# DeltaNet with a channel mixer on one core: the first channel product of the last batch for 768 tokens at once, in 11 products for 12

## The chip, the core and the metric

The kernel runs on one NeuronCore of a Trainium2 chip. The core has TensorE (PE, matrix products, with its weight loads shown apart as PEld), VectorE (DVE), ScalarE (ACT), GpSimd (POOL), SyncE (SP, which only starts transfers here) and 16 DMA engines. They run side by side and wait for each other by semaphores. TensorE reads SBUF and writes PSUM, which has eight banks of 512 float32 columns; VectorE and ScalarE take results out of PSUM.

The metric is the device time of one execution in microseconds; the median of several runs is given.

## What is computed

Four batches of 768 tokens pass through DeltaNet (8 heads of width 48), and the result, 384 wide, through a mixer:

```python
y[:, :, t] = np.einsum('bhd,bhde->bhe', q[:, :, t], state)      # DeltaNet, for t in range(768)
v_old = np.einsum('bhde,bhd->bhe', state, kt)
state = state + bt[:, :, :, None] * np.einsum('bhd,bhe->bhde', kt, vt - v_old)
...
x = y.transpose(0, 2, 1, 3).reshape(4, 768, 384)
h = x.transpose(0, 2, 1) @ U @ V                                # token mixing, rank 32
u = x + h.transpose(0, 2, 1)
out = u + np.maximum(u @ w_ch1, 0.0) @ w_ch2                    # 384 -> 1536 -> 384
```

The change concerns the last line, for the last batch: `u @ w_ch1`, called the first channel product here. `@ w_ch2` is the second.

## The kernel before

All arithmetic is float32. DeltaNet is computed in units of half a batch, eight in all; the working set of a unit lies in one of two SBUF slots (`slots`, 9792 columns each), units taking them in turn. The mixer takes a batch in three groups of 256 tokens (`GT`, `NG`). For each group:

- `front(b, i)` (line 1030) mixes tokens: `x += v @ tt` (line 1054, 384 columns, summed on VectorE in line 1058), six transposes (line 1062), and a copy by ScalarE into `ut` (line 1065). It works in blocks of 128 tokens.
- `wide(b, i)` (line 1080) makes the first channel product (line 1132): 12 feature blocks of 128, each 3 products of a 128x128 weight block with 256 tokens. Two feature blocks share a PSUM bank, from which `relu` (line 1088) writes `hs`.
- Then it makes the second channel product (line 1169) by the seven products of a Strassen-Winograd scheme, each a sum over 6 weight blocks of 192 columns. `add_up` (line 1104) and `last_sum` (line 1111) make the sums of `hs` that it needs, in `S1`, `S2` and `hs`; the sums of weights were made at the start. `gather` (line 1117) adds results to `X` and starts the store of 128 tokens by SP (line 1121).

The order of instructions isn't written out by hand. Every part is a generator that yields the operations it wants to issue (engine, estimated cost, PSUM banks to take or give back) and the keys it waits for (`need`); `run` (line 209) keeps a clock for each engine and picks the next operation by place, the number that `begin` gives to a part. Fronts have place 2, `wide` 95; a table, `PLACES`, gives other places to some parts. The result is a fixed program with a fixed order on each engine. PSUM is handed out as four `pair`s of two banks; once the first batch is ready the last pair is taken away and split into two single banks, `mix`, for the channel products.

In the last batch no DeltaNet is left to run beside the mixer.

Of the kernel before, what the change touches and what calls it, by code (L numbers as in the profile page):

```python
# [8 lines left out]
FP32 = mybir.dt.float32  # L9
# [10 lines left out]
GT = 256  # L20
# [6 lines left out]
def kernel(  # L27
# [66 lines left out]
    def dve(n):  # L94
        return (n + 151) / 960.0
# [14 lines left out]
    def need(*keys):  # L110
        return [key for key in keys if key[1] >= 0]
# [232 lines left out]
    v_sb = const.tile([128, S], FP32, name="v_sb")  # L344
    w2_sb = const.tile([128, PRODUCTS, HF, HD], FP32, name="w2_sb")
    hs = const.tile([128, FT, GT], FP32, name="hs")
    S1 = const.tile([128, HF, 128], FP32, name="S1")
    S2 = const.tile([128, HF, 128], FP32, name="S2")
    X = const.tile([128, 2, NB, DM], FP32, name="X")
# [574 lines left out]
    def sums(f):  # L924
# [3 lines left out]
            nc.vector.tensor_tensor(out=w[:, to], in0=w[:, a], in1=w[:, c], op=ALU.subtract)  # L928
        emitted(("sums", f), 0.2)

    def load_weights():
        landed = {}
        slices = list(weight_slices())
        room = X.bitcast(I32).rearrange("p a b d -> p a (b d)")[:, 1]
        wides = [
            room[:, 0 : 2 * WIDE],
            conv.tile([128, 2 * WIDE], I32, name="wide", bufs=1),
            hs.bitcast(I32).rearrange("p f n -> p (f n)")[:, 0 : 2 * WIDE],
        ]
        where = [0, 1, 0, 1, 2, 0, 1, 2, 0, 1, 0, 1, 0, 1]  # L940
        uppers, powers = room[:, 2 * WIDE :], conv.tile([128, WIDE], I32, name="power", bufs=1)
# [36 lines left out]

        yield need(("seeded", 0))
        for i in range(len(slices)):  # L980
            begin(start(i), 22)
        for i in range(len(slices)):
            dst, n = slices[i][0], size(i)
            yield need(("wide", i))
            yield op("dve", 0.15 + n / 1850, port=True)
            wide = landed.pop(i)
            h, low = wide[:, :, 1], wide[:, :, 0].bitcast(U32)
            power, upper = powers[:, 0:n], uppers[:, 0:n]
            nc.vector.tensor_scalar(
                out=power, in0=h, scalar1=20, scalar2=0x7FF,  # L990
                op0=ALU.logical_shift_right, op1=ALU.bitwise_and,
            )
# [24 lines left out]
            nc.vector.scalar_tensor_tensor(  # L1017
                out=dst, in0=mant, scalar=2.0 ** -20, in1=power, op0=ALU.mult, op1=ALU.mult
            )
            emitted(("weights", i), 0.1)  # L1020
            if i >= W2 + 4:
                begin(sums(3 * (i - W2 - 4)), 21)

    uts, tts = {}, {}
    NG = S // GT

    def before(b, i):
        return (b, i - 1) if i > 0 else (b - 1, NG - 1)

    def front(b, i):  # L1030
        yield need(
            ("front", *before(b, i)), ("wide", *before(*before(b, i))),
            ("weights", 1), *[("x", b, c) for c in range(NC)],
        )
        x = X[:, b % 2]
# [13 lines left out]
        ut = uts[b, i] = mix.tile([128, KT, GT], FP32, name="ut")  # L1049

        def block(c):
            o = yield op("pe", 0.65, "F", take="pair", words=4)
# [25 lines left out]
        emitted("mixing")  # L1078

    def wide(b, i):  # L1080
        yield need(("front", b, i), ("narrow", *before(b, i)))
        x, ut = X[:, b % 2], uts[b, i]
        if b == 0 and i == 0:
            yield ["mixing"]

# [6 lines left out]
        def part(k, m, f0, n=3):  # L1092
            return hs[:, k * HF + f0 : k * HF + f0 + n, 128 * m : 128 * m + 128]

        def add_up(f0, fs):
            yield need(*[("h", b, i, x) for x in fs])
# [17 lines left out]
        def gather(m, p, c, h, last):  # L1114
            yield op("dve", dve(HD), give=[("mix", m)])
            to = x[:, NT * i + c, HD * h : HD * h + HD]
            nc.vector.tensor_tensor(out=to, in0=to, in1=p, op=ALU.add)  # L1117
            if last:
                yield op("sp", 0.4)
                at = (NT * i + c) * 128  # L1120
                nc.sync.dma_start(out=out[b, at : at + 128, :], in_=x[:, NT * i + c])
                emitted(("stored", b, NT * i + c), 2.0)

        firsts = []
        for y, fs in enumerate(PAIRS):
            yield need(("weights", 2 + y))
            for f in fs:
                got = yield op("pe", 1.3, "F", take="mix" if f == fs[0] else None, words=12)
# [19 lines left out]

        banks = {}
        for y, (w, a, keys, bank, first, c, h, last) in enumerate((  # L1150
            (0, part(0, 0, 0, HF), [("h", b, i, x) for x in ((3, 4), (5, 9))] + [("weights", W2 + 2)],
             0, True, 0, 0, False),
            (1, part(1, 0, 0, HF), [("h", b, i, (10, 11)), ("weights", W2 + 5)], 1, True, 0, 0, False),
            (5, S2, [("summed", b, i, 0), ("summed", b, i, 3), ("sums", 0), ("sums", 3)],
             0, False, 0, 1, False),
            (4, S1, [], 1, True, 1, 1, False),
# [17 lines left out]
            begin(gather(m, p_o, c, h, last), 3)  # L1174
        emitted(("narrow", b, i))

    with tc.manual_schedule():
# [13 lines left out]
                    begin(load(n, name, (0, 1)), FIRST.get((name, n), 20 + 4 * n + y))  # L1191
        begin(load_weights(), 40)
        begin(reserve(), 0)
        for b in range(B):
            for i in range(NG):
                begin(front(b, i), 2)
# [34 lines left out]
```

## Time and profile before

| quantity | value |
|---|---|
| median of 3 runs | 621.54 us (621.28 to 623.51) |
| the profiled execution | 622.19 us |
| its span, first to last instruction | 620.1 us |
| mean granted TensorE clock | 0.939 |
| ScalarE, Relu of line 1088, 128x512 | 72 times, 597 ns |
| VectorE, sum of line 1104, 128x384 | 72 times, 551 to 559 ns |
| VectorE, gather of line 1117, 128x192 | 84 times, 350 ns |
| stores of 192 KB (line 1121), issue to landing | 24 times, median 1.9 us |

The page of a profile gives busy time of each engine, the same in 40 slices of the span, and groups of equal instructions: line, engine, operation, what it writes and reads, how often, busy time and mean, then the idle time of the engine just before such instructions and who ended it. The chain of waits is followed back from the last instruction, at each step to what released it. Timelines list instructions by start and length. The time of an execution is some 2 us longer than its span. TensorE's matrix records overlap, so the pace of a series is read from starts, not from the mean length.

### The profile page before, as it was taken

The numbers are of one execution on the slowest core, as the hardware profiler recorded it, in microseconds if no ns is written. First come the engines' busy times: TensorE is split into PE (matmuls) and PEld (weight loads), VectorE is DVE, ScalarE is ACT, GpSimd is POOL, SyncE is SP. The second block draws the span as 40 slices with busy tenths as digits, with TensorE's granted clock in tenths as the row PEclk, the third lists the DMA queues.
The fourth block names the chain that finished last, engine by engine and source line by source line (L and its number), as shares of the span: only waits on it lengthen the run. The fifth ranks groups of instructions, "written<-read, shape, count | busy, mean of one in ns | idle before, by whom it ended". The sixth has DMA issues, their size and how long they took to land.

```text
span 620.1 us, 23438 instructions
## 1 busy us (share of the span) xinstructions
PE 589.1 (95%) x10536; PEld 518.6 (84%) x10536; DVE 401.0 (65%) x965; ACT 228.3 (37%) x450; POOL 82.5 (13%) x145
## 2 busy tenths in 40 slices
PE   6678988999999999999999999999999999999997
PEld 5578976789888878799889878889889869898987
DVE  5869997898989613889898128898894123131312
ACT  3465564740342553521621643245324321101020
POOL 3011052410010343200100511401001000000000
PEclk9766565999999999999999999999999999999999
DMA  9840568850000332410000611600000000000000
GB/s 146 159 88 5 177 177 177 186 123 14 15 4 29 64 75 52 77 37 0 30 3 13 113 41 30 133 2 3 30 3 14 16 3 9 18 5 21 15 12 25
DMA packets 72004, 33.26 MB, mean 54 GB/s; under 512 B 59616, under 2 KB 70368, under 8 KB 71904
## 3 DMA queue, kind: packets, MB, share of 16 engines
q1 hardware_dynamic: 66112, 24.98, 18.3%
q0 software_dynamic: 4192, 6.49, 4.6%
q8 instruction: 82, 1.34, 0.9%
q10 hardware_dynamic: 1600, 0.30, 0.3%
q14 instruction: 18, 0.15, 0.1%
HBM read 27.03 MB, written 4.72 MB: 51 GB/s over the span
## 4 chain that ended last, share of the span: by engine, by line
PE 82%; DVE 9%; SPq 5%; issue 2%; DMA 1%; ACT 0%; ACTq 0%; DVEq 0%
PE P L1132 30%; PE P L1169 27%; SPq L382 4%; PE P L505 3%; PE P L478 2%; PE P L860 2%; PE P L1054 2%; PE P L775 2%; PE P L888 2%; PE P L811 2%; PE P L789 2%; DVE prod L596 1%; DVE xt L602 1%; PE P L822 1%; PE P L666 1%
## 5 line engine op out<-in xcount | busy, mean ns | idle before, releaser
L1132 PE MATMUL P<-ut,w_sb 128*128 128x256 f32 x864 | 201.9, 385 | 0.0
L1132 PEld LDWEIGHTS P<-ut,w_sb 128*128 128x128 f32 x864 | 159.4, 190 | 22.4 <-issue 0.6
L1169 PE MATMUL P<-w_sb,hs 128*128 128x192 f32 x720 | 125.6, 329 | 0.0
L1169 PEld LDWEIGHTS P<-w_sb,hs 128*128 128x128 f32 x720 | 117.1, 190 | 3.9 <-issue 1.2
L1088 ACT ACTIVATE hs<-P 128x512 f32<-128x512 f32 x72 | 43.0, 597 | 167.1 <-PE P L1132 163.1
L1117 DVE TENSOR_TENSOR X<-X,P 128x192 f32<-128x192 f32 x84 | 29.4, 350 | 62.7 <-PE P L1169 62.1
L602 DVE TENSOR_TENSOR xt<-xt,prod 128x112 f32<-128x112 f32 (+21 forms) x200 | 64.6, 323 | 6.9
L596 DVE TENSOR_TENSOR prod<-gs,xt 128x112 f32<-128x112 f32 (+21 forms) x200 | 64.1, 321 | 4.8
L759 ACT COPY X<-P 64x192 f32<-64x192 f32 x96 | 30.1, 313 | 71.3 <-PE P L789 54.6
L1169 PE MATMUL P<-w_sb,S 128*128 128x192 f32 x288 | 50.5, 329 | 0.0
L1169 PEld LDWEIGHTS P<-w_sb,S 128*128 128x128 f32 x288 | 46.8, 190 | 0.6
L1104 DVE TENSOR_TENSOR S<-hs 128x384 f32<-128x384 f32 x24 | 13.2, 552 | 52.4 <-ACT hs L1088 52.3
L873 DVE TENSOR_TENSOR z<-slot,P 128x192 f32<-128x192 f32 x44 | 15.5, 352 | 45.6 <-PE P L860 30.8
L478 PE MATMUL P<-ident,slot 128*128 128x128 f32 x192 | 30.4, 309 | 13.4 <-DMA slot<-in_k_dram 11.4
L478 PEld LDWEIGHTS P<-ident,slot 128*128 128x128 f32 x192 | 25.0, 158 | 18.3 <-issue 13.2
L731 ACT COPY slot<-zz 32x384 f32<-32x384 f32 x64 | 32.5, 509 | 12.2 <-DVE zz L609 7.9
L493 ACT COPY slot<-P 128x768 f32<-128x768 f32 x30 | 23.7, 803 | 31.1 <-PE P L478 30.9
L581 POOL MEMSET xt<- 128x1056 f32 x8 | 7.8, 980 | 186.7 <-DVE zz L609 186.7
L505 PE MATMUL P<-slot 48*64 48x64 f32 x1536 | 31.8, 238 | 0.5 <-ACT slot L493 0.2
L505 PEld LDWEIGHTS P<-slot 48*64 48x64 f32 x1536 | 28.7, 150 | 3.9 <-ACT slot L493 2.1
L738 POOL MEMSET slot<- 32x384 f32 x32 | 13.6, 424 | 108.6 <-PE P L695 63.0
L382 POOL DMA_DIRECT2D slot<-in_k_dram x36 | 24.2, 679 | 28.1 <-PE P L888 28.1
(119 smaller groups left out, 780.7 us busy)
## 6 DMA issues: line engine op xcount, KB each, us to landing
out_dram<-X SPq DMA_DIRECT2D x24, 192.0 KB, 1.9
slot<-in_k_dram SPq DMA_DIRECT2D x56, 72.0 KB, 4.0
X<-in_moe_w_ch_dram SPq DMA_DIRECT2D x10, 384.0 KB, 5.5
wide<-in_moe_w_ch_dram SPq DMA_DIRECT2D x10, 384.0 KB, 5.1
slot<-in_q_dram SPq DMA_DIRECT2D x40, 72.0 KB, 3.6
slot<-in_v_dram SPq DMA_DIRECT2D x40, 72.0 KB, 2.7
slot<-in_k_dram POOLq DMA_DIRECT2D x36, 72.0 KB, 3.9
slot<-in_q_dram POOLq DMA_DIRECT2D x24, 72.0 KB, 4.6
```

The source lines that it names most:

```text
L382: queue.dma_start(out=t[half(1 - g if name == "z" else g), :, to, 0:D], in_=src[b, 4 * g + s, hf * UC * L : (hf + 1) * UC * L, :].rearrang ...
L478: nc.tensor.transpose(p_t[:, c // 3, c % 3], t[:, c, 2 * j : 2 * j + 2].rearrange("p s d -> p (s d)"), ident,)
L493: nc.scalar.copy(to, p_t)
L505: nc.tensor.matmul(p_g[half(g ^ (par * i)), par, c], kq[rows, c, j, 0, half(g)], kq[rows, c, j, i, half(g)], start=True, stop=True,)
L596: nc.vector.tensor_tensor(out=prod, in0=gb[:, :, j : j + 1, j + 1 :].to_broadcast([128, split, m, w]), in1=xb[:, :, 0:m, j : j + 1].to_bro ...
L602: nc.vector.tensor_tensor(out=xb[:, :, 0:m, j + 1 :], in0=xb[:, :, 0:m, j + 1 :], in1=prod, op=ALU.subtract,)
L731: nc.scalar.copy(pg[quarter(i), :, at, :, a : a + BK], cut(zc, h)[quarter(i)].rearrange("p r (c j) t -> p r c j t", j=2),)
L759: nc.scalar.copy(x[half(c % 2), c // 2, 4 * D * g : 4 * D * (g + 1)].rearrange("p (j r d) -> p r j d", r=2, d=D), states(p_y)[half(g)],)
L1088: nc.scalar.activation(hs[:, fs[0] : fs[1] + 1 : fs[1] - fs[0]], p_f, ACTF.Relu)
L1117: nc.vector.tensor_tensor(out=to, in0=to, in1=p, op=ALU.add)
L1132: nc.tensor.matmul(p_f[:, fs.index(f)], w1_sb[:, y, 256 * t + 128 * fs.index(f) :][:, 0:128], ut[:, t], start=(t == 0), stop=(t == KT - 1),)
L1169: nc.tensor.matmul(p_o, a[:, f], w2_sb[:, w, f], start=(first and f == 0), stop=(f == HF - 1), skip_group_check=True,)
```

## The change

For the last batch, the first channel product is no longer made by group. `first_of_last` waits for the fronts of all three groups, then starts `quick(f)` for f = 0 to 5. Each makes four results of 128 features by 384 tokens: feature blocks f and f + 6 (k = 0, 1), token halves m = 0, 1. The inner dimension has three blocks of 128. Over the first two, 2x2 blocks are multiplied in 7 products for 8; the third adds 4; so 11 products of 384 columns stand for 12. Partial results are copied by ScalarE from PSUM into `hs_last` and added to there by VectorE, and the Relu is then made in place by ScalarE (`cut`), or straight from PSUM for one of the four.

`hs_last` (12 x 768 columns) lies in slot 0 and `ut_last` with the sums of tokens in slot 1, whose units are finished by then. Sums of weights lie in the two buffers used for the conversion of the weights at the start (`converted`, `exponents`), apart from one that takes the place of a weight block. `weight_sums` makes the first 18 of them once all weights are in and the second channel product of batch 1's first group has been issued, and the last six when batch 2 is through its last first product. `token_sums` makes five sums of 384 columns.

The front of the last batch no longer waits for an earlier `wide`. The second channel product is the same, from `hs_last`. For the very last group the results are stored by halves of columns, each as soon as it is final, four transfers for two.

In the built program the order on every engine is as before up to the last batch, apart from the 24 sums of weights on VectorE: 18 stand between lines 618 and 873 soon after the first group of batch 1, six among lines 1046 to 1117 at the end of batch 2. From the fork on, TensorE's order is: the blocks of the last 256 tokens, moved ahead between the last products of batch 2; the 66 products of `quick`; then three times the second channel product, the first of its seven in front of the last two products of `quick`.

```diff
+    LAST = B - 1
+    hs_last = slots[0][:, 0 : FT * S].rearrange("p (f n) -> p f n", f=FT)
+    ut_last = slots[1][:, 0 : KT * S].rearrange("p (t n) -> p t n", t=KT)
+    ts_last = slots[1][:, KT * S : KT * S + 2 * S].rearrange("p (z n) -> p z n", z=4)
+    w1_sums = [converted.bitcast(FP32)[:, 0:WIDE], converted.bitcast(FP32)[:, WIDE:]]
+    w1_sums = [t.rearrange("p (f x) -> p f x", f=HF) for t in w1_sums + [exponents.bitcast(FP32)]]
...
+    def weight_sums():
+        yield need(("weights", W2 + 5), ("narrow", 1, 0))
+        for f in range(HF):
+            a11, a12, a21, a22 = (w1_of(f + HF * k, t) for k in range(2) for t in range(2))
+            n1, s2, s4 = (t[:, f] for t in w1_sums)
+            for to, a, c, sign in ((n1, a21, a22, -1.0), (s2, n1, a11, -1.0), (s4, a12, s2, 1.0)):
+                yield op("dve", dve(128), port=True)
+                nc.vector.scalar_tensor_tensor(
+                    out=to, in0=a, scalar=sign, in1=c, op0=ALU.mult, op1=ALU.subtract
+                )
+        emitted(("w1 sums", 1), 0.1)
+        yield need(("wide", LAST - 1, NG - 1))
+        for f in range(HF):
+            yield op("dve", dve(128), port=True)
+            a21 = w1_of(f + HF, 0)
+            nc.vector.tensor_tensor(out=a21, in0=w1_of(f, 0), in1=a21, op=ALU.subtract)
+        emitted(("w1 sums", 0), 0.1)
...
+    def quick(f):
...
+        def cut(k, m):
+            yield op("act", act(384))
+            nc.scalar.activation(c(k, m), c(k, m), ACTF.Relu)
+            emitted(("cut", k, m, f), 0.06)
+
+        def add(k, m, p, **more):
+            yield op("dve", dve(384), rush=True, **more)
+            nc.vector.tensor_tensor(out=c(k, m), in0=c(k, m), in1=p, op=ALU.add)
+            begin(cut(k, m), 3)
...
+        x = yield op("pe", 0.65, "F", take="pair", words=4)
+        px, pz = (pair(x)[:, z, 0:384] for z in range(2))
+        mm(px, w1_of(f, 0), u(0, 0), start=True, stop=True)
+        begin(copies(), 3)
+        yield need(("tokens", 0), ("w1 sums", 1))
+        yield op("pe", 0.65, "F", words=4)
+        mm(pz, n1, t1, start=True, stop=True)
+        emitted(("fifth", f), 0.22)
+        y = yield op("pe", 1.3, "F", take="mix", words=8)
+        py = mixed(y)[:, 0:384]
+        mm(py, w1_of(f, 1), u(1, 0), start=True)
+        mm(py, w1_of(f, 2), u(2, 0), stop=True)
+        emitted(("other", f), 0.22)
+        begin(first(y), 3)
+        yield need(("begun", f))
+        yield op("pe", 0.65, "F", words=4)
+        mm(px, s2, t2, stop=True)
+        begin(second(), 3)
+        yield need(("third", f))
+        yield op("pe", 1.3, "F", words=8)
+        mm(pz, s4, u(1, 1))
+        mm(pz, w1_of(f, 2), u(2, 1), stop=True)
+        emitted(("both", f), 0.22)
+        begin(both(), 3)
+        yield need(("second", f), ("w1 sums", 0))
+        yield op("pe", 1.3, "F", words=8)
+        mm(px, w1_of(f + HF, 0), u(0, 1))
+        mm(px, w1_of(f + HF, 2), u(2, 1), stop=True)
+        yield from add(1, 1, px)
+        yield op("pe", 1.3, "F", words=8)
+        mm(px, w1_of(f + HF, 1), t4)
+        mm(px, w1_of(f + HF, 2), t5, stop=True)
...
     def wide(b, i):
-        yield need(("front", b, i), ("narrow", *before(b, i)))
-        x, ut = X[:, b % 2], uts[b, i]
+        yield need(("front", b, i), ("half" if b == LAST else "narrow", *before(b, i), *[3] * (b == LAST)))
+        x, hs = X[:, b % 2], hidden
+        if b == LAST:
+            hs = hs_last[:, :, GT * i : GT * i + GT]
+        else:
+            ut = uts[b, i]
...
-            if last:
+            at = (NT * i + c) * 128
+            if b == LAST and i == NG - 1:
+                if final:
+                    yield op("sp", 0.4)
+                    cols = slice(HD * h, HD * h + HD)
+                    nc.sync.dma_start(out=out[b, at : at + 128, cols], in_=x[:, NT * i + c, cols])
+            elif last:
                 yield op("sp", 0.4)
-                at = (NT * i + c) * 128
                 nc.sync.dma_start(out=out[b, at : at + 128, :], in_=x[:, NT * i + c])
...
-        for y, fs in enumerate(PAIRS):
+        if b == LAST:
+            for f0 in range(0, HF, 3):
+                begin(add_up(f0, ()), 4)
+            yield need(("narrow", *before(b, i)))
+        for y, fs in enumerate(PAIRS if b < LAST else ()):
```

In the order of `quick`, the small letters of the code stand for these products of a block f, in the order in which they are issued: A is the first (into `px`), B the one with `n1` (into `pz`), then the two into `py`, E the one with `s2`, F the two with `s4` and `w1_of(f, 2)`, G the two in front of `add(1, 1, px)`, H the two behind it.

More of the change, by code (lines that the diff above doesn't have):

```diff
@@ L346 @@
     hs = const.tile([128, FT, GT], FP32, name="hs")
+    hidden = hs
     S1 = const.tile([128, HF, 128], FP32, name="S1")
@@ L929, in sums @@
         emitted(("sums", f), 0.2)
+    converted = conv.tile([128, 2 * WIDE], I32, name="wide", bufs=1)
+    exponents = conv.tile([128, WIDE], I32, name="power", bufs=1)
     def load_weights():
@@ L936, in load_weights @@
             room[:, 0 : 2 * WIDE],
-            conv.tile([128, 2 * WIDE], I32, name="wide", bufs=1),
+            converted,
             hs.bitcast(I32).rearrange("p f n -> p (f n)")[:, 0 : 2 * WIDE],
@@ L940, in load_weights @@
         where = [0, 1, 0, 1, 2, 0, 1, 2, 0, 1, 0, 1, 0, 1]
-        uppers, powers = room[:, 2 * WIDE :], conv.tile([128, WIDE], I32, name="power", bufs=1)
+        uppers, powers = room[:, 2 * WIDE :], exponents
         def size(i):
@@ L1022, in load_weights, with w1_of @@
                 begin(sums(3 * (i - W2 - 4)), 21)
+    LAST = B - 1
[4 more added lines that the diff above has]
+    w1_sums = [t.rearrange("p (f x) -> p f x", f=HF) for t in w1_sums + [exponents.bitcast(FP32)]]
+    def w1_of(f, t):
+        y = [f in fs for fs in PAIRS].index(True)
+        return w1_sb[:, y, 256 * t + 128 * PAIRS[y].index(f) :][:, 0:128]
@@ new lines, in token_sums @@
+    def token_sums():
+        yield need(*[("front", LAST, i) for i in range(NG)])
+        u = ut_last.rearrange("p t (m n) -> p t m n", m=2)
+        t1, t2, t4, t5 = (ts_last[:, z] for z in range(4))
+        for to, a, c, how in (
+            (t1, u[:, 0, 0], u[:, 0, 1], ALU.subtract),
+            (t2, u[:, 1, 1], t1, ALU.add),
+            (u[:, 0, 1], u[:, 1, 1], u[:, 0, 1], ALU.subtract),
+            (t4, u[:, 1, 0], t2, ALU.subtract),
+            (t5, u[:, 2, 0], u[:, 2, 1], ALU.subtract),
+        ):
+            yield op("dve", dve(384), port=True)
+            nc.vector.tensor_tensor(out=to, in0=a, in1=c, op=how)
+        emitted(("tokens", 0), 0.1)
@@ new lines, in quick, with u, c, mm @@
+    def quick(f):
+        n1, s2, s4 = (t[:, f] for t in w1_sums)
+        t1, t2, t4, t5 = (ts_last[:, z] for z in range(4))
+        def u(t, m):
+            return ut_last[:, t, 384 * m : 384 * m + 384]
+        def c(k, m):
+            return hs_last[:, f + HF * k, 384 * m : 384 * m + 384]
+        def mm(to, w, t, start=False, stop=False):
+            nc.tensor.matmul(to, w, t, start=start, stop=stop, skip_group_check=True)
+        def cut(k, m):
[6 more added lines that the diff above has]
+            begin(cut(k, m), 3)
+        def first(y):
+            yield need(("begun", f), ("other", f))
+            yield from add(0, 0, py, give=[("mix", y)])
+        def copies():
+            yield op("act", act(384), rush=True)
+            nc.scalar.copy(c(0, 0), px)
+            emitted(("begun", f), 0.06)
+            yield need(("fifth", f))
+            yield op("act", act(384), rush=True)
+            nc.scalar.copy(c(1, 1), pz)
+            emitted(("third", f), 0.06)
+        def second():
+            yield op("act", act(384), rush=True)
+            nc.scalar.copy(c(0, 1), px)
+            emitted(("second", f), 0.06)
+        def both():
+            yield need(("both", f), ("second", f))
+            yield from add(0, 1, pz)
+            emitted(("out", f))
+        x = yield op("pe", 0.65, "F", take="pair", words=4)
[30 more added lines that the diff above has]
+        mm(px, w1_of(f + HF, 2), t5, stop=True)
+        emitted(("quick", f))
+        yield op("act", act(384), rush=True)
+        nc.scalar.activation(c(1, 0), px, ACTF.Relu)
+        emitted(("cut", 1, 0, f), 0.06)
+        yield need(("out", f))
+        free["pair"][x] = state["now"] + 0.06
@@ L1024, with first_of_last @@
+    def first_of_last():
+        yield need(*[("front", LAST, i) for i in range(NG)], ("narrow", LAST - 1, NG - 1))
+        for f in range(HF):
+            begin(quick(f), 94)
     uts, tts = {}, {}
@@ L1031, in front @@
         yield need(
-            ("front", *before(b, i)), ("wide", *before(*before(b, i))),
+            ("front", *before(b, i)), *[("wide", *before(*before(b, i)))] * (b < LAST),
             ("weights", 1), *[("x", b, c) for c in range(NC)],
@@ L1048, in front @@
         cs = list(range(i * GT // 128, (i + 1) * GT // 128))
-        ut = uts[b, i] = mix.tile([128, KT, GT], FP32, name="ut")
+        if b < LAST:
+            ut = uts[b, i] = mix.tile([128, KT, GT], FP32, name="ut")
+        else:
+            ut = ut_last[:, :, GT * i : GT * i + GT]
         def block(c):
@@ L1080, in wide @@
     def wide(b, i):
-        yield need(("front", b, i), ("narrow", *before(b, i)))
-        x, ut = X[:, b % 2], uts[b, i]
+        yield need(("front", b, i), ("half" if b == LAST else "narrow", *before(b, i), *[3] * (b == LAST)))
+        x, hs = X[:, b % 2], hidden
+        if b == LAST:
+            hs = hs_last[:, :, GT * i : GT * i + GT]
+        else:
+            ut = uts[b, i]
         if b == 0 and i == 0:
@@ L1093, in part, with cut_off @@
             return hs[:, k * HF + f0 : k * HF + f0 + n, 128 * m : 128 * m + 128]
+        def cut_off(ks, fs):
+            ms = ((0,), (0, 1), (1,))[i]
+            return [("cut", k, m, f) for k in ks for m in ms for f in fs] if b == LAST else []
         def add_up(f0, fs):
-            yield need(*[("h", b, i, x) for x in fs])
+            yield need(*[("h", b, i, x) for x in fs], *cut_off(range(2), range(f0, f0 + 3)))
             at = slice(f0, f0 + 3)
@@ L1112, in last_sum, with gather @@
             emitted(("summed", b, i, 6), 0.1)
-        def gather(m, p, c, h, last):
+        def gather(m, p, c, h, last, final):
             yield op("dve", dve(HD), give=[("mix", m)])
@@ L1150, in wide @@
         for y, (w, a, keys, bank, first, c, h, last) in enumerate((
-            (0, part(0, 0, 0, HF), [("h", b, i, x) for x in ((3, 4), (5, 9))] + [("weights", W2 + 2)],
+            (0, part(0, 0, 0, HF),
+             cut_off((0,), range(HF)) or [("h", b, i, (3, 4)), ("h", b, i, (5, 9)), ("weights", W2 + 2)],
              0, True, 0, 0, False),
-            (1, part(1, 0, 0, HF), [("h", b, i, (10, 11)), ("weights", W2 + 5)], 1, True, 0, 0, False),
+            (1, part(1, 0, 0, HF),
+             cut_off((1,), range(HF)) or [("h", b, i, (10, 11)), ("weights", W2 + 5)],
+             1, True, 0, 0, False),
             (5, S2, [("summed", b, i, 0), ("summed", b, i, 3), ("sums", 0), ("sums", 3)],
@@ L1173, in wide @@
             emitted(("half", b, i, y))
-            begin(gather(m, p_o, c, h, last), 3)
+            begin(gather(m, p_o, c, h, last, y in (1, 4, 5, 6)), 3)
         emitted(("narrow", b, i))
@@ L1193 @@
         begin(reserve(), 0)
+        begin(weight_sums(), 97)
+        begin(token_sums(), 3)
+        begin(first_of_last(), 94)
         for b in range(B):
```

## The prediction

> **What bounds the kernel now.** I read the page first (busy shares, then the slices), then the chain of waits, then the timelines of the last 120 us, then the last transfer.
>
> ```profile
> PE 589.1 (95%) x10536; PEld 518.6 (84%) x10536; DVE 401.0 (65%) x965; ACT 228.3 (37%) x450; POOL 82.5 (13%) x145
> PEclk9766565999999999999999999999999999999999
> ...
> L1132 PE MATMUL P<-ut,w_sb 128*128 128x256 f32 x864 | 201.9, 385 | 0.0
> ```
>
> TensorE is busy 95% of the span, it runs at full clock from the ninth slice on, and the matmuls of the first channel product (line 1132) have no idle time in front of them. The records come in twos: one product in the code gives two passes, each with its own weight load. The chain of waits from 500 us on shows where the change sits:
>
> ```profile
> 519.61 7.80 PE P L1169 x48
> 527.41 15.54 PE P L1132 x72
> 542.95 1.29 PE P L1054 x4
> 544.24 1.95 PE P L1169 x12
> 546.19 0.65 PE P L1062 x6
> 546.84 11.70 PE P L1169 x72
> 558.55 15.54 PE P L1132 x72
> 574.09 13.65 PE P L1169 x84
> 587.74 15.54 PE P L1132 x72
> 603.28 13.66 PE P L1169 x84
> 616.94 0.02 issue
> 616.97 0.35 DVE X L1117
> ```
>
> Each row is start, length, what. From 507 to 617 us the path is TensorE alone: one piece starts where the last ended. Three first products of 256 tokens (line 1132) take 15.54 each. The page's mean of 385 ns is no price, since records overlap. The pace is 15.54/72 = 0.2158 us for a pass of 256 columns, 1.95/12 = 0.1625 for 192 columns, 1.29/4 = 0.3225 for 384 columns (line 1054). So time removed from TensorE here is time off the end, if nothing new makes it wait. The two other engines are mostly idle there:
>
> ```profile
> 520.00:540.00 20.00, 20.00 (x106) 18.48 (x105) 3.01 (x7) 2.56 (x5) 0.00 (x0) 1.00 0.05 20
> 580.00:600.00 20.00, 20.00 (x106) 18.53 (x105) 3.33 (x8) 2.39 (x4) 0.00 (x0) 1.00 0.06 20
> ```
>
> (PE, weight loads, VectorE, ScalarE, GpSimd, clock.) Three rows of the timelines give the price of a handover:
>
> ```profile
> 590.41 0.60 ACT L1088 ACTIVATE hs<-P 128x512 f32<-128x512 f32 x1 [15.63 <-PE P L1132]
> 504.61 0.35 DVE L873 TENSOR_TENSOR z<-slot,P 128x192 f32<-128x192 f32 x1 [1.75 <-PE P L860]
> 505.02 0.45 PE L789 MATMUL P<-z,slot 64*64 64x48 f32 x16 [0.24 <-DVE z L873]
> ```
>
> The first pair of blocks ends its 12 passes at 587.74 + 12 x 0.2158 = 590.33, and ScalarE starts 0.08 later. VectorE ends at 504.96 and TensorE starts 0.06 later. A mean record of 0.385 at a pace of 0.216 has 0.17 of drain; the chain's starts already stand after it, but I add it once, to be safe. The round trip TensorE, ScalarE, TensorE for 384 columns is then at most 0.17 + 0.08 + 0.48 (line 488, 480 ns) + 0.06 = 0.79 us, and over VectorE with 0.55 (line 1058) 0.86.
>
> **What the skill says.** "TensorE: Matmul & The Clock Gate", section "Back-to-back issue gap", gives columns/2.4 GHz plus 2.5 ns. The trace agrees, with two cycles a column for each of the two float32 passes: 256 x 2/2.4 + 2.5 = 215.8 ns, 384 columns 322.5. Its "Step-by-step: what each phase is for" says that weight loads are pulled ahead of running matmuls; a load has 190 ns here, under the 322 of the new passes. "DMA: Bandwidth & Descriptors", in "Anatomy of one DMA", makes most of a small transfer a fixed cost of about 2 us; the 192 KB stores land in 1.9, so that order holds. "SBUF — State Buffer", section "Who interferes with whom", says that a VectorE instruction with two SBUF inputs gets in the way of GpSimd instructions that read SBUF, not of those that only write. The trace agrees for issuing: four POOL transfers at 397.25 took 2.62 us beside such VectorE work, 0.66 each, as everywhere.
>
> **The change part by part.**
>
> *The product.* Removed: 3 x 72 passes at 0.2158 = 46.62 us. Added: 6 blocks x 11 products x 2 passes = 132 passes at 0.3225 = 42.57. Both are path. **Gain 4.05.** The pace of 384 columns is measured on four passes only; drawn on from 192 and 256 columns it would be 0.2158 + 2 x 0.0533 = 0.3224, so the bounds lie within 0.1 us in all.
>
> *New waits in the product.* The order of TensorE's instructions is unchanged up to the last batch-2 product. Then a block f stands in the queue as A (1 product), B (1), H of the block before (2), other (2), E (1), F (2), G (2). G accumulates on what ScalarE copies out after E: between lies F, four passes, 4 x 0.3225 = 1.29 against 0.79: 0.50 to spare. H needs VectorE's sum after G: A and B lie between, 1.29 against 0.86: 0.43 to spare. E and F wait on copies over three products old or more. Behind a late G or H all of TensorE would stand. On ScalarE one block asks 4 instructions from PSUM at 0.48 and 3 in SBUF at 0.48 to 0.61 (line 628), at most 3.8 us of the block's 22 x 0.3225 = 7.1; VectorE 3 x 0.55 and, from block 2 on, the sums of line 1104, moved. The first of these waits in VectorE's queue for a Relu, with block 3's first sum behind it; that one frees a PSUM bank which TensorE takes again two blocks later. At the end of block 5 H stands behind a product of six weight blocks (1.95 > 0.86); the next product waits for the last Relu only at its sixth weight block, 5 x 2 x 0.1625 = 1.62 later, against 0.79, and the one after it at its fourth block for two sums behind that Relu: 1.95 + 0.98 against 0.79 + 2 x 0.56 + 0.1. I take zero; the bounds are zero and 12 handovers x 0.2 = 2.4, as if each were 0.65 late.
>
> *Fronts.* The blocks of the last 256 tokens (4 passes of line 1054, 6 of 1062) move from 543 us to before the last three batch-2 products. Same instructions, 0. VectorE then has five token sums at 0.55 among the gathers. The first waits for the copy of the transposes, with a gather behind it that frees a PSUM bank. The copies end 0.57 after the transposes (519.61 to 520.18), two sums make 1.75, and the gather's product ends 1.95 after them: on time.
>
> *Weight sums.* 18 instructions of 128 columns; nearest row 128x192 at 324 ns (line 1017), at most that, 5.8 us in all. They stand where VectorE idles 14.1 us from 344 on. Three come in front of a state sum at 342.51 and make it 0.3 late; its consumer runs at 357.8. Six more (at most 0.28 each) fit in gaps of 1.59 and 1.78 us at 509 and 514. Zero. If that cover went, GpSimd's transfers of 344 to 351 us could slip: the tensors of 350.4 are transposed at 355.7 and land 4.5 to 5.0 after issue, which leaves about 0.5. Bounds: 0 to 2 us.
>
> *Last store.* Today 2.78 us lie between the last VectorE instruction (617.32) and the end. The transfer itself is visible:
>
> ```profile
> 618.00:618.25 0.25, 0.00 (x0) 0.00 (x0) 0.00 (x0) 0.00 (x0) 0.00 (x0) 1.00 0.11 43
> 618.25:618.50 0.25, 0.00 (x0) 0.00 (x0) 0.00 (x0) 0.00 (x0) 0.00 (x0) 1.00 0.98 375
> 618.50:618.75 0.25, 0.00 (x0) 0.00 (x0) 0.00 (x0) 0.00 (x0) 0.00 (x0) 1.00 0.94 350
> ```
>
> 192 KB take some 0.55 us; the last issue then carries 96 KB, with SP's three others out 1.95 us or more before. I take half, **0.25**; bounds 0 (if shorter rows move more slowly) and 0.3.
>
> Sum: 4.05 + 0.25 = 4.3. On the profiled execution: span 620.1 to 615.8, 622.19 to 617.9 (2.1 lies around the span). The median shown is 621.54, 0.65 below that execution: 621.54 - 4.3 = **617.2 us**.
>
> **Rivals.**
> 1. *TensorE waits partly in the new product.* For it: the spare 0.43 is thin, and ScalarE serves in order, so a copy can stand behind a Relu that waits for VectorE. Against: ScalarE is half idle. 12 handovers late by 0.2 leave 1.9 of gain: about 619.6; with half of them 618.4.
> 2. *The handovers take the product over: slower.* Place: every G and H. Price: from a round trip of 1.29 on, each further microsecond costs 12 us; at 1.29 + 4.3/12 = 1.65 the gain is gone, that is twice what I measure. If a copy regularly stood behind one Relu and one more sum (0.6 + 0.55 more, 2.0 in all) it would cost 12 x 0.7 = 8.5: 625.7. Against: the instruction ahead of G's copy on ScalarE, the Relu of H of the block before, can start 0.25 after H and is done 0.73 after it, 1.2 before E ends.
> 3. *The weight sums delay loads at 344 to 351.* Cost 1 to 2 us on the path, 618.4 to 619.2. Against: rates of issue beside VectorE as above.
> 4. *It doesn't do what it says* (12 products, or a scattered order): about 621.3. Against: the built order has 66 products for 108, and one mass of them.
>
> **How the numbers follow.** Forecast 0.80, rival 1 0.09, rival 2 0.05, rival 3 0.05, rival 4 0.01. The forecast's own spread is 616.4 to 618.0: tail bounds, and medians of three that move by some 0.5. The range goes to 619.0, which takes in rivals where half the cost is met. A measurement of this kernel tells 0.5% (3.1 us) from no change. Faster (under 618.4): all but a little of the forecast, half of rivals 1 and 3, 0.85. Same: rest of these and rival 4, 0.09. Slower: rival 2 with a little beyond, 0.06.
>
> **What would show it.** One run of TensorE of 132 passes in about 42.6 us with no idle before it, starting near 529.4 (527.4 and the 1.95 us of fronts moved ahead); its pieces touching in the chain; the stretch from there to the last matmul at 42.6 + 3 x 13.65 = 83.5 instead of 89.5 less those 1.95; the last gather to the end at 2.5. Wrong if TensorE idles before G or H "<- ACT" or "<- DVE", if passes take more than 0.33, or if the span before 515 us is longer.

## The result and the profile after

The changed kernel takes 618.67 us (median of 9 runs, 616.78 to 619.67) against 621.54 us of the kernel before (9 runs, 619.98 to 623.68). The ratio is 0.9944, with a 95% interval of 0.9925 to 0.9964: 3.5 us faster by the means, 2.2 to 4.7 by the interval. In a second series the same program took 617.57 (6 runs) against 622.13 us (39 runs), ratio 0.9920 (0.9892 to 0.9948). The profiled execution took 619.43 us and its span is 617.7.

First the page of the changed kernel, the lines that answer to those shown of before:

```profile
PE 587.0 (95%) x10452; PEld 504.5 (82%) x10452; DVE 418.8 (68%) x1012; ACT 237.0 (38%) x474; POOL 82.5 (13%) x145
...
PEclk9656555899999999999999999999999999999999
...
L1296 PE MATMUL P<-ut,w_sb 128*128 128x256 f32 x648 | 154.8, 387 | 0.0
...
L1089 PE MATMUL P<-slot,w_sb 128*128 128x384 f32 x96 | 33.3, 486 | 0.0
```

216 passes of 256 columns are gone from the old product (864 to 648); the new one is at line 1089 (96 passes whose weights lie in `w_sb`; 36 more, with sums of weights in the two conversion buffers, are in other groups). Neither has idle time in front of it. TensorE is as busy as before, VectorE and ScalarE took on work: the bound is the same engine. The chain of waits of the changed kernel at its end (start, length, what):

```profile
...
527.03 3.90 PE P L1336 x24
530.93 41.28 PE P L1089 x128
572.21 1.95 PE P L1336 x12
574.16 1.29 PE P L1089 x4
575.45 39.01 PE P L1336 x240
614.46 0.02 issue
614.49 0.35 DVE X L1272
```

The 132 passes take 41.28 + 1.29 = 42.57 us, and every piece starts where the last ended. From the start of the product to the last matmul it is 614.46 - 530.93 = 83.53 us. The last transfer (start and end of the slice, its length, five engines, clock, share of the DMA engines, GB/s), in the changed kernel:

```profile
615.50:615.75 0.25, 0.00 (x0) 0.00 (x0) 0.00 (x0) 0.00 (x0) 0.00 (x0) 1.00 0.10 37
615.75:616.00 0.25, 0.00 (x0) 0.00 (x0) 0.00 (x0) 0.00 (x0) 0.00 (x0) 1.00 0.97 326
616.00:616.25 0.25, 0.00 (x0) 0.00 (x0) 0.00 (x0) 0.00 (x0) 0.00 (x0) 1.00 0.11 31
```

Its 96 KB move in about 0.4 us; the last byte is through at 616.12, 1.28 us after the last gather. The semaphore that tells of the landing arrives at 616.46, and the span ends at 617.73, another 1.27 us later.

How the handover in front of G stands is seen in the timelines of one block of the changed kernel (start, length, instruction, in brackets the idle time before it):

```profile
547.54 0.81 PE L1089 MATMUL P<-slot,wide 128*128 128x384 f32 x2
548.18 0.81 PE L1089 MATMUL P<-slot,power 128*128 128x384 f32 x2
548.83 2.74 PE L1089 MATMUL P<-slot,w_sb 128*128 128x384 f32 x8
...
548.38 0.48 ACT L1116 COPY slot<-P 128x384 f32<-128x384 f32 x1 [1.45 <-PE P L1089]
...
550.96 0.56 DVE L1098 TENSOR_TENSOR slot<-slot,P 128x384 f32<-128x384 f32 x1 [0.67 <-PE P L1089]
```

E is the pair of passes at 547.54, F the four from 548.18 on, so G starts at 549.47. ScalarE's copy is done at 548.86. VectorE's sum after G is done at 551.52, and H starts at 552.05 (the two pairs of A and B lie between). Both handovers are in time; the engines wait for TensorE, not the other way round.

### The profile page after: what moved, and what is told of

Read it like the earlier page. It is cut to its first block, busy times and chain, and to the rows that moved or that the text cites. A ratio compares the mean times of both kernels' runs of the same rounds, so it can differ in the third digit from the quotient of the medians.

```text
span 617.7 us, 23345 instructions
## 1 busy us (share of the span) xinstructions
PE 587.0 (95%) x10452; PEld 504.5 (82%) x10452; DVE 418.8 (68%) x1012; ACT 237.0 (38%) x474; POOL 82.5 (13%) x145
## 4 chain that ended last, share of the span: by engine, by line
PE 83%; DVE 9%; SPq 4%; issue 2%; DMA 1%; ACT 1%; DVEq 0%; ACTq 0%
PE P L1336 27%; PE P L1296 23%; PE P L1089 7%; PE P L506 3%; SPq L383 3%; PE P L479 3%; PE P L1201 2%; PE P L667 2%; PE P L861 2%; PE P L653 2%; PE P L776 2%; PE P L812 2%; PE P L889 1%; DVE prod L597 1%; DVE xt L603 1%
## 5 line engine op out<-in xcount | busy, mean ns | idle before, releaser
L1296 PE MATMUL P<-ut,w_sb 128*128 128x256 f32 x648 | 154.8, 387 | 0.0
L1296 PEld LDWEIGHTS P<-ut,w_sb 128*128 128x128 f32 x648 | 118.4, 190 | 17.0 <-issue 0.6
L1336 PE MATMUL P<-w_sb,hs 128*128 128x192 f32 x540 | 95.4, 330 | 0.0
L1336 PEld LDWEIGHTS P<-w_sb,hs 128*128 128x128 f32 x540 | 87.6, 190 | 3.8 <-issue 1.2
L1239 ACT ACTIVATE hs<-P 128x512 f32<-128x512 f32 x54 | 32.2, 597 | 97.8 <-PE P L1296 94.8
L1089 PE MATMUL P<-slot,w_sb 128*128 128x384 f32 x96 | 33.3, 486 | 0.0
L1336 PE MATMUL P<-w_sb,slot 128*128 128x192 f32 x180 | 30.1, 326 | 0.0
L1336 PEld LDWEIGHTS P<-w_sb,slot 128*128 128x128 f32 x180 | 29.4, 190 | 0.5
```

The source lines that it names most:

```text
L1089: nc.tensor.matmul(to, w, t, start=start, stop=stop, skip_group_check=True)
L1239: nc.scalar.activation(hs[:, fs[0] : fs[1] + 1 : fs[1] - fs[0]], p_f, ACTF.Relu)
L1296: nc.tensor.matmul(p_f[:, fs.index(f)], w1_sb[:, y, 256 * t + 128 * fs.index(f) :][:, 0:128], ut[:, t], start=(t == 0), stop=(t == KT - 1),)
L1336: nc.tensor.matmul(p_o, a[:, f], w2_sb[:, w, f], start=(first and f == 0), stop=(f == HF - 1), skip_group_check=True,)
```

## Where the time went: two stretches

The order of instructions is the same in both kernels up to the first sum of weights. VectorE's last transposes ahead of it (line 618 before, 619 after) are therefore a landmark that divides the span: what lies ahead of it is the same work in both. It varies by itself: the nine profiles with a changed last batch have the landmark from 338.19 to 341.76, on both sides of the two before (all times in us from the span's start).

| kernel | landmark | landmark to last matmul | last gather to end |
|---|---|---|---|
| before | 339.93 | 277.01 | 2.80 |
| before, second profile | 339.35 | 276.97 | 2.79 |
| changed | 341.47 | 272.99 | 2.89 |
| changed, second profile | 339.83 | 273.12 | 2.90 |

From the landmark on, the change gains 3.94 us (276.99 against 273.05 on average over the profiles of kernels with the same arithmetic: these two and four below). In the first pair of profiles 1.54 of the gain was covered up by a later landmark. Its origin lies in the first 44 us. The timelines of VectorE and of SP's queue in the kernel before:

```profile
16.71 5.38 SPq L382 DMA_DIRECT2D slot<-in_k_dram  x7
...
31.77 11.54 SPq L382 DMA_DIRECT2D slot<-in_v_dram  x16
...
40.05 1.36 DVE L461 TENSOR_TENSOR slot<-slot,norm_rows 128x1152 f32<-128x1152 f32 x1 [4.45 <-DMA slot<-in_v_dram]
```

and the same rows of the changed kernel:

```profile
16.63 7.96 SPq L383 DMA_DIRECT2D slot<-in_k_dram  x7
...
33.10 11.42 SPq L383 DMA_DIRECT2D slot<-in_v_dram  x16
...
41.63 1.36 DVE L462 TENSOR_TENSOR slot<-slot,norm_rows 128x1152 f32<-128x1152 f32 x1 [5.89 <-DMA slot<-in_v_dram]
```

Seven equal transfers of `k` took SP 7.96 us to issue instead of 5.38; the twelve issues that follow made up for some of it, so that the first of `v` went out 1.33 later, and VectorE, which waits for `v`, started 1.58 later. From there to the landmark both kernels take 299.9 us, so this is all of the 1.54. In the eleven profiles VectorE's start follows SP's first issue of `v` after 7.4 to 8.7 us, while that issue itself lies anywhere from 29.7 to 33.1. The part from there to the landmark varies too, from 298.8 to 303.3. The longest belongs to the run with eleven stores, where VectorE started early (38.47) and the landmark is the latest of all (341.76); there TensorE's mean granted clock between 20 and 50 us was 0.50, against 0.56 to 0.66 in the other ten profiles. So the loads aren't the only thing that moves the early part. Why SP's issues are slower in some executions, and what the clock adds, these traces don't show.

## Experiments

All ratios are to the kernel before, measured on the same chip in the same series.

**The unchanged product at the new place.** `quick` makes 12 plain products of 384 columns; sums of weights and of tokens, copies and additions are left out.

```diff
-        x = yield op("pe", 0.65, "F", take="pair", words=4)
...
+        for k in range(2):
+            x = yield op("pe", 1.95, "F", take="pair", words=12)
+            for m in range(2):
...
+                for t in range(KT):
+                    nc.tensor.matmul(
+                        p, w1_of(f + HF * k, t), u(t, m), start=(t == 0), stop=(t == KT - 1)
+                    )
+                begin(result(k, m, x, p), 3)
...
-        begin(weight_sums(), 97)
-        begin(token_sums(), 3)
```

> The last batch's first channel product for all 768 tokens at once, but as 12 plain products of 384 columns, with no sums of weights or tokens (all of the result is still computed). Theory A (the gain is TensorE passes alone, and what the median lacks was lost before the first changed instruction by the clock's phase): the product takes 144 passes x 0.3225 = 46.4 us for 42.6, so from the last VectorE transpose before the first sums of weights (339.9 before, 341.5 after) to the last matmul it is 3.9 longer than the changed kernel and 0.2 shorter than before. Theory B (the sums of weights in the middle cost part of the gain): the stretch from that transpose to the start of the product gets shorter than in the changed kernel by 0.5 us or more.

Measured: 622.39 us, ratio 0.9994 (0.9977 to 1.0012). The chain of waits of this kernel:

```profile
531.29 46.44 PE P L1097 x144
...
618.69 0.02 issue
```

144 passes take 46.44 us, 0.3225 each: of the product's gain 3.87 us come from the twelfth product that is saved (46.44 - 42.57), and 0.18 from wider passes (46.62 - 46.44). Staying with 12 products and only widening them is not told from no change. Theory A is right on the product, but missed the stretch from the landmark to the last matmul: 277.63, which is 0.6 longer than before where 0.2 shorter was expected, and 0.77 more than 3.87 explains. The surplus lies between the landmark and the start of the product (190.23 us against 189.46), a part with the same instructions in the same order as before and without any sum of weights; so it speaks against theory B, and such a stretch can vary by that much. Theory A's words on the clock's phase are not needed for the first pair, where the late loads account for all of the 1.54.

**The last store whole.** Only the store of the last group is put back to whole rows.

```diff
-            if b == LAST and i == NG - 1:
+            if b == LAST and i == NG:
```

> The changed kernel with the last group's stores whole again, two of 192 KB for four of 96. Theory A, as the prediction priced it: the end comes 0.25 later after the last gather than with halves. Rival: the wait for the landing varies more than the 0.25 of transfer that is saved, and the time from the last gather to the end is the same within 0.1 to 0.3 (2.8 to 2.9 us in both profiles so far).

Measured: 618.26 us, ratio 0.9935 (0.9911 to 0.9959), landmark to last matmul 273.04, last gather to end 2.79 against 2.89 with halves. The halves gain nothing, so theory A falls. The rival has the number, but not the reason: the landing of the last store varies little. It comes 1.88 us after the last gather with whole stores (here and in the second profile of the kernel before) and 1.62 with halves. Where the 0.26 that this gains is lost again is seen below, under the last two runs.

**The sums of weights at the end of batch 2.** The first 18 sums wait for the same point as the last six.

```diff
-        yield need(("weights", W2 + 5), ("narrow", 1, 0))
+        yield need(("weights", W2 + 5), ("wide", LAST - 1, NG - 1))
```

> The 18 sums of weights moved from the middle (342 to 350 us) to the end of batch 2, where VectorE also idles. Theory A: nothing changes, the stretch from the last transpose before the old place to the last matmul is 273.0 us as in the changed kernel (614.5 - 341.5), within 0.1. Theory B (the sums cost time where they stand, through the state sum or GpSimd's transfers beside them): that stretch gets shorter by 0.5 us or more.

Measured: 618.62 us, ratio 0.9945 (0.9922 to 0.9968), landmark to last matmul 272.86, that is 0.13 less than in the changed kernel, which is also what its two profiles differ by. No cost of the sums where they stand is seen, and theory B, which asked for 0.5 or more, falls; nothing speaks for rival 3.

**The changed kernel once more**, for a second profile and a second series.

> The changed kernel once more, unchanged. Theory A: the last transpose before the first sums of weights comes anywhere within 339 to 342 us, and from there to the last matmul it is 273.0 us again within 0.1. Theory B says the same of the stretch; if the stretch itself varies by 0.5 or more, neither holds and the later part has a variation of its own.

Measured: 617.57 us, ratio 0.9920 (0.9892 to 0.9948), landmark 339.83, stretch 273.12: 0.13 from the first profile, a little over the 0.1 that was expected, and far from 0.5.

**The kernel before once more.**

> The kernel before, unchanged, for a second profile of it. My theory, that the start of the late part moves by over a microsecond from one execution to the next and that the part behind it is fixed: landmark (VectorE's last transpose ahead of the first changed instruction) anywhere between 338 and 342, landmark to last matmul 277.0 within 0.7, which is what the profiles so far show for such jitter, last matmul to end 3.2. Rival, that 277.0 was one draw of a stretch that moves as much as the early part: outside 276.3 to 277.8.

Measured: 621.78 us, ratio 0.9996 (0.9979 to 1.0014), landmark 339.35, stretch 276.97, last matmul to end 3.17, all as the theory has it.

**A longer handover.** ScalarE's copy between E and G is made twice.

```diff
-            nc.scalar.copy(c(0, 1), px)
+            for _ in range(2):
+                nc.scalar.copy(c(0, 1), px)
```

> ScalarE's copy that stands between E and G of every block is issued twice (the second time over the first, same result). Measured in the changed kernel, the copy starts 0.19 us after E's products have been drained and is done some 0.6 us before G needs it. One more copy adds 0.38 (the pace of ScalarE's instructions, if their fixed ends overlap) to 0.48 us (the whole instruction). My theory, that 0.5 to 0.6 us of slack is real: still no TensorE idle in the product, 42.57 us on the chain for its 132 passes, stretch from VectorE's last transpose before the first changed instruction to the last matmul 273.0 as in the changed kernel, within 0.2, median as the changed kernel's 618.5 within its spread. Rival (the handover was already at its edge): 6 waits of 0.3 to 0.5, product 44.4 to 45.5, stretch 274.8 to 276.

Measured: 616.83 us, ratio 0.9922 (0.9888 to 0.9956); product 41.63 + 1.29 = 42.92, 0.35 more than without; stretch 273.50. The expectation was missed by a little, and the reason is in the timelines of ScalarE and of the weight loads of this kernel:

```profile
545.52 0.99 ACT L1117 COPY slot<-P 128x384 f32<-128x384 f32 x2 [1.44 <-PE P L1089]
...
546.56 1.59 PEld L1089 LDWEIGHTS P<-slot,w_sb 128*128 128x128 f32 x6 [0.41 <-ACT slot L1117]
```

Two copies into the same place take 0.99, so the second adds 0.51 and not 0.38 to 0.48. And it is the weight load of G that waits: it starts 0.41 after the end of the load before it, instead of 0.13 as in the undisturbed series. The load stands one pass (0.32) ahead of the pass that needs it. It started 0.27 late, of which 0.06 a block (0.35/6) reached the passes.

**A much longer handover.** The copy is made four times.

```diff
-            nc.scalar.copy(c(0, 1), px)
+            for _ in range(4):
+                nc.scalar.copy(c(0, 1), px)
```

> The same copy four times in a row. Three more copies add 1.14 to 1.44 us to a handover with 0.5 to 0.6 to spare. My theory: G waits 0.55 to 0.9 in each of six blocks, all of it on the path: product 42.57 + 3.3 to 5.3 = 45.9 to 47.9, stretch from the landmark to the last matmul 276.3 to 278.3, and the gain over the kernel before is used up: about 621 to 624. Rival (ScalarE's extra work is taken by slack elsewhere, as its queue is half empty): no more than 1 us on the stretch.

Measured: 624.46 us, ratio 1.0037 (1.0019 to 1.0055), stretch 279.34. The chain of waits of this kernel, one block:

```profile
542.35 6.09 PE P L1089 x18
...
548.46 0.49 ACT slot L1117
548.97 0.49 ACT slot L1117
...
550.00 0.49 ACT slot L1117
...
550.53 6.09 PE P L1089 x18
```

A block lasts 8.18 us instead of 22 x 0.3225 = 7.095, so 1.085 of three copies (3 x 0.51 = 1.53) is on the path: 0.445 was to spare. Six blocks make 6.5 us, and the product is 49.05 (579.85 - 528.85, less 1.95 of the second product inside). The expectation had the mechanism, and its rival falls, but the sizes were missed: the product came to 49.05 where 45.9 to 47.9 was expected, and the stretch to 279.34 where 276.3 to 278.3 was, because three copies add 1.53 and not 1.14 to 1.44, and 0.445 is to spare and not 0.5 to 0.6. This is rival 2 brought about: nothing behind the wait takes it up, and the changed kernel falls behind the kernel before. The two runs agree: 0.51 - 0.445 = 0.065 a block, and 0.06 was found with two copies.

**What the last store waits for.** From the last byte that moves to the end it is 1.3 us with whole stores and 1.6 with halves. Two theories were put: each of the last stores adds a fixed piece, or the form of the last one does. In the first kernel the first half store of the group is cut into eight:

```diff
-                    nc.sync.dma_start(out=out[b, at : at + 128, cols], in_=x[:, NT * i + c, cols])
+                    step = 128 if c or h else 16
+                    for r in range(0, 128, step):
...
```

> Of the last group's four half stores the first one, which is issued some 9.7 us before the last, is cut into eight pieces of 16 tokens; the last store, its issue and all arithmetic stay as they are. In the profiles so far the last byte moves 1.46 us after VectorE's last gather with two whole stores and 1.23 with four halves, but from the last byte to the end it is 1.32 with whole and 1.63 with halves. Theory of number: each store of the last group adds a fixed piece to the end, 0.31/2 = 0.155 us; 11 stores for 4 then make 1.63 + 7 x 0.155 = 2.7 from the last byte to the end, and 4.3 for 3.25 from the last matmul to the end. Theory of shape: the last store's own form (halves of rows) makes it end later after its last byte; then nothing changes: 1.63 and 3.25, within 0.1.

In the second the first 128 tokens are stored whole:

```diff
-            if b == LAST and i == NG - 1:
+            if b == LAST and i == NG - 1 and c == 1:
```

> The first 128 of the last 256 tokens are stored whole, the last 128 by halves: three stores for four, the last one (96 KB) unchanged. Theory of number: 1.63 - 0.155 = 1.47 from the last byte to the end, 3.1 from the last matmul. Theory of shape: 1.63 and 3.25, within 0.1.

Measured, one execution each, which tells nothing about gains: 620.14 us with eleven stores, 618.68 with three, 621.37 for the kernel before. Stretches from the landmark: 273.35 and 272.96. From the last gather to the end it takes 2.96 and 2.95, from the last matmul 3.33 in both, from the last byte 1.67 in both. The theory of number, which wanted 2.7 and 1.47 for the last of these, falls. The theory of shape has its numbers, but the traces show another cause.

At the end of the program SP waits for its transfers, one semaphore after the other. There are eight of them, in a fixed order, and the transfers that SP issues take them in turn. The rows below are SP's instructions of the program's last line from the landing of the last store on (line, engine, operation, how many, shortest, median and longest in ns, start of the first and the last); the first is the wait for that store itself, and two in each row belong to the handover between engines that closes the program. First the changed kernel, then the one with whole stores, then the one with eleven stores:

```profile
L1396 SPq EVENT_SEMAPHORE  x9: 17/28/28, 616.5 to 617.7; - x9
```

```profile
L1396 SPq EVENT_SEMAPHORE  x3: 17/17/28, 613.5 to 614.3; - x3
```

```profile
L1401 SPq EVENT_SEMAPHORE  x10: 17/28/28, 617.1 to 618.4; - x10
```

With whole stores the last store has the eighth semaphore of the row: SP has passed the other seven waits before it lands, and the span ends 0.90 us after the landing. With halves there are two more stores, so the last one has the second semaphore, and six waits are still to be passed, though all that they wait for has long come. They take 0.06 each, and the end comes 1.27 after the landing. With eleven stores, and with three, the last store has the first semaphore; seven waits follow, and with eleven the end comes 1.33 after the landing (with three its time isn't recorded). Seven stores more and one store fewer are the same place in a round of eight, so this pair of runs couldn't tell number from form. The form is not the cause: from the last byte to the landing it is 0.34 with halves and with whole stores.

## Why the prediction was right, step by step

*The product: exact.* 4.05 us were forecast. 46.62 became 42.57; the pace of 0.3225 us for 384 columns, taken from four passes, held for 132 here and for 144 in the run with 12 products. This is also the formula of the Trainium skill that the prediction used ("TensorE: Matmul & The Clock Gate", "Back-to-back issue gap"), and the trace agrees with it to the last digit shown, with two passes of two cycles a column for each float32 product. The page gives the formula for a matmul by itself and says that a stream of wide matmuls runs faster than it; the stream of 132 passes here doesn't, and the measurement decides.

*Waits in the product: none, as taken.* TensorE doesn't idle, and the stretch from the start of the product is 83.53 for 83.5. The slack before G was put at 0.50; lengthening the copy showed 0.445. The round trip is then 1.29 - 0.445 = 0.845 us and not at most 0.79. The term left out is the weight load: that "Step-by-step" of the same page has loads pulled ahead of running matmuls was used for saying that loads don't limit, not for what waits. It is the load that waits, a pass early, as the run with two copies shows. The pieces in the run with four copies fit: 0.19 from the end of E by its pace to the first copy, 0.49 for a copy and 0.05 from its end to the load make 0.73, and the 0.12 that is missing is most likely the load itself, in front of the first pass. Since a load of 0.19 has 0.32 to itself, some of its lateness is still hidden: of 0.27 in the run with two copies 0.21 was. Rival 2 asked for a round trip beyond 1.29; with four copies it is 0.845 + 1.53 = 2.375, and the 6.5 us lost came from G's six handovers alone (the rival had counted twelve). Slack in front of H wasn't tried; VectorE's sum ended 0.53 before H's pass, 0.21 before its weight load, in the block shown.

*Fronts and sums of weights: zero, as taken.* The chain has the same fronts, moved (1.29 us from 523.13 and 0.65 from 526.37, as from 542.95 and 546.19 before), and the product starts at 530.93, which is the 529.4 that was forecast plus the later landmark. Moving the 18 sums away changed the stretch by 0.13, as much as a repeat did.

*The last store: the step that failed.* Half of the 0.55 us of moving bytes, 0.25, was taken, with bounds of 0 and 0.3. The transfer itself did what was worked out: the last store landed 0.26 sooner after the last gather (1.62 us for 1.88). But the prediction took what lies behind the landing to be the same for every store, and there SP's six further waits cost 0.37 (1.27 us for 0.90). From the last gather to the end it became 2.89 where 2.5 was forecast, so the term is -0.09 and lies outside its lower bound. As an estimate from these numbers, with the last store at the end of the row it would have been 2.89 - 0.37 = 2.52; no run here tried that.

*The sum.* 4.3 was forecast and 3.93 is what the first pair of profiles gives from the landmark to the end (280.19 to 276.26): 4.02 less 0.09. Against that stand 1.54 of later loads, and 0.37 less around the span: 622.19 - 3.93 + 1.54 - 0.37 = 619.43. The medians show the same wandering: 618.67 and 617.57 for one program. That the first of them lies in the range is partly luck: it is above the forecast's own spread (616.4 to 618.0), and the range reached to 619.0 because it takes in rivals at half their cost, of which the traces have no sign. By the number alone, half of rival 1 (618.4) would have looked as good; it is the chain without gaps that tells them apart. The forecast of 617.2 from a base of 621.54 took the start as constant; the prediction gave "some 0.5" to such movements, and the landmarks of eleven profiles lie between 338.19 and 341.76. Among its signs of error was a longer span before 515 us. It was longer, but ahead of the first changed instruction; from the landmark on the part up to the product took no longer, so that sign should have been stated from there.

## What to carry to other kernels

Where the bounding engine's passes follow each other without gaps, a product saved was worth its pass time to the digit here, as long as every handover that the cheaper scheme adds is shorter than the products put between. A late handover met the weight load first, one pass ahead of the pass itself, and some 0.2 us of the load's lateness stayed hidden; reading the slack from the passes gave 0.50, and 0.445 was there. Lengthening one handover on purpose measures this slack better than reading it. To compare two profiles of a long kernel, divide the span at the last instruction that both share, since the part ahead of it moved here by almost as much as the whole gain. And when the number of stores at the end changes, look at what the program does between the last landing and its end: an earlier landing was lost there to waits that had nothing left to wait for.

## What the runs showed that was not expected

- The start of this kernel moves by up to 3.6 us between executions of the same instructions (landmark 338.19 to 341.76). Part of it, and all of the 1.54 in the first pair, comes from SP's issues of the first loads, which take different times (5.2 to 8.0 us for seven equal transfers).
- Halving the last store brought its landing 0.26 us forward and the end of the kernel 0.1 back: 2.89 to 2.96 us from the last gather to the end in eight profiles with halves, 2.79 to 2.80 in three with whole rows. What decides is the place of the last store's semaphore in SP's closing row of eight: eighth, second or first leaves no, six or seven waits at 0.06 us each.
- A ScalarE copy that writes what the copy before it wrote starts only after that one has ended: 0.51 us from one copy to the next, where the copy itself has 0.48 to 0.49. Two copies of the same size into different places start 0.38 apart in these traces (line 1065 before: 0.86 us for two).
